# Loading order, weight piece width and one add moved between engines, at the start of a fused attention and gated-FFN kernel

## The chip, the cores and the metric

The kernel runs on one core of a Trainium2 chip. A core has a matrix engine (TensorE, PE in the profile; its weight loads are PEld), VectorE (DVE), ScalarE (ACT), GpSimd (POOL), a queue engine that issues the loads and stores (SyncE, SP), and sixteen DMA engines that carry them. The metric is the device time of one execution in microseconds; lower is better. The time before is 222.35 us, the median of 3 runs (222.17 to 222.53).

## The reference

The input is 2048 tokens of 512 features, in bf16. It is normalized over the features, and two branches read the result: linear attention with 32 heads of 16, whose queries and keys go through a small matrix per head and a pair of softmaxes, and a gated bilinear feed-forward net with 1792 hidden features. The output is the input plus both branches.

```python
xn = _layernorm(x, axis=-1)
return x + _A_ref(xn, A_wqkv, A_w_phi, A_wo) + _B_ref(xn, B_w_gate, B_w_up, B_w_down)

# _A_ref
q, k, v = split(x @ wqkv)
pq, pk = q @ w_phi, k @ w_phi                    # per head, 16 x 16
phi_q = concat(softmax(pq), softmax(-pq)); phi_k = concat(softmax(pk), softmax(-pk))
kv = sum over s of phi_k^T v;  z = sum over s of phi_k
o = (phi_q @ kv) / (phi_q @ z + 1e-6)
return o @ wo

# _B_ref
return ((x @ w_gate) * (x @ w_up)) @ w_down
```

## The kernel before

Tokens are worked on in 16 tiles of 128; four tiles make a group. The 512 features are four chunks of 128, and a product over the features is four matmuls that add up in one PSUM bank. There are six banks in rotation for all short-lived results (`bank`), and a bank that is asked for waits for whoever still reads its last content.

The order of instructions on each engine is the order in which the code issues them (`manual_schedule`): nothing is reordered, and an instruction that waits holds all that stand behind it on its engine. All loads are issued on the sync queue at the top (L84 to L99), in the order written there. A load may not be issued before the one eight places ahead of it has landed.

The part that the change touches is the start, where the first group of tiles (0 to 3, tokens 0 to 511) goes through:

- Statistics and scaling on VectorE: `first_stats` computes a tile's sums (`bn_stats`, L155), then, where `amid` names a tile, scales that tile (`first_apply`, L171), and then makes mean and variance (`bn_aggr`, L347). `ln_rstd` adds epsilon to the variance (L164) and raises it to the power -0.5 (L166), both on GpSimd. The order on VectorE is: sums 0, aggregate 0, sums 1, aggregate 1, scale 0, sums 2, scale 1, aggregate 2, sums 3, scale 2, aggregate 3, scale 3, and then `make_bd` (L221), which needs the small matrices `wphi`.
- `lt(n)` transposes a scaled tile on TensorE (four transposes, L213), and ScalarE copies it to `xnT` (L215; in two halves for tiles 0 and 1).
- `vproj(n)` multiplies a tile with `wv` (L240, the result is called pv). Its first two matmuls need the first half of `wv`, the others the second half; between the halves, `amid` lets the transposes of another tile in. ScalarE evicts the results of tiles 0 and 1 (L322), VectorE those of tiles 2 and 3.
- `unit(T, f, lo, hi)` makes one chunk f of 128 hidden features for the tokens lo to hi of group T: four matmuls with `wg` into a bank g, four with `wu` into a bank u (L275); ScalarE casts g to bf16 (L279), VectorE multiplies u with it (L280). At the start, units 0 and 1 are made in two halves of 256 tokens, since only tiles 0 and 1 are there at first. From then on a unit covers 512 tokens.

TensorE's order at the start is: 10 matmuls on zeros, transposes 0, one more on zeros, half of pv 0, transposes 1, the other half, pv 1, transposes 2, unit 0 (tokens 0 to 255), half of pv 2, transposes 3, the other half, unit 1 (tokens 0 to 255), pv 3, the second halves of units 0 and 1, unit 2, the fold of `wphi` into the key weights (L231), and further units with the key products between them.

The weights `wg` and `wu` are loaded in slices of columns: `dma_gu(lo, hi)` loads chunks lo to hi of both. A slice of 256 columns is carried in pieces of 512 bytes, one of 512 columns in pieces of 1 KB.

Of the kernel before, what the change touches and what calls it, by code (L numbers as in the profile page):

```python
# [8 lines left out]
BF16 = mybir.dt.bfloat16  # L9
F32 = mybir.dt.float32  # L10
AF = mybir.ActivationFunctionType
ALU = mybir.AluOpType
# [9 lines left out]
def kernel(  # L22
# [12 lines left out]
    nc = tc.nc  # L35
    P = 128
    S, D = A_x.shape[-2], A_x.shape[-1]
# [4 lines left out]
    DC = D // P  # L42
    FC = F // P
    EPS = 1e-5
    GT = 4
    NGRP = NT // GT
    TT = GT * P
# [16 lines left out]
    wv = wpool.tile([P, DC, D], BF16)  # L64
    wphi = consts.tile([P, DC, DH], BF16)
    wg = wpool.tile([P, DC, F], BF16)
    wu = wpool.tile([P, DC, F], BF16)
# [6 lines left out]
    def dma_x(lo, hi):  # L74
        nc.sync.dma_start(out=xall[:, lo:hi, :], in_=x_view(lo, hi))

    def dma_cols(eng, w, src, lo, hi, at=0):
        eng.dma_start(out=w[:, :, lo - at:hi - at], in_=src[:, lo:hi].rearrange("(c p) f -> p c f", p=P))

    def dma_gu(lo, hi):  # L80
        dma_cols(nc.sync, wg, B_w_gate, lo * P, hi * P)
        dma_cols(nc.sync, wu, B_w_up, lo * P, hi * P)

    dma_x(0, 1)  # L84
    dma_x(1, 2)
    dma_x(2, 4)
    for lo in (0, 2):
        nc.sync.dma_start(out=wv[:, lo:lo + 2, :],
                          in_=A_wqkv[lo * P:(lo + 2) * P, 2 * D:3 * D].rearrange("(c p) f -> p c f", p=P))
    dma_gu(0, 2)  # L90
    nc.sync.dma_start(out=wphi[:], in_=A_w_phi.rearrange("(c h) d f -> (h d) c f", c=DC))
    dma_gu(2, 4)
    nc.sync.dma_start(out=wT2[:, 1, :, :], in_=A_wqkv[:, D:2 * D], transpose=True)
    dma_gu(4, 9)
    dma_x(4, 8)
# [29 lines left out]
    xnT = xpool.tile([P, DC, S], BF16)  # L125
# [15 lines left out]
    gpool = ctx.enter_context(tc.tile_pool(name="gpool", bufs=3))  # L141
# [6 lines left out]
    def bank(name, dt=F32, n=TT):  # L148
        return ps_s.tile([P, n], dt, name=name, tag="s")
# [9 lines left out]
        stats = ln_sums(n)  # L159
        nc.vector.bn_aggr(out=mv, in_=stats[:])  # L160

    def ln_rstd(mv, k):
        ve = lnpool.tile([P, GT], F32, name="ve")
        nc.gpsimd.tensor_scalar(out=ve[:, 0:k], in0=mv[:, 0:k, 1], scalar1=EPS, scalar2=None, op0=ALU.add)  # L164
        rstd = lnpool.tile([P, GT], F32, name="rstd", bufs=GT)
        nc.gpsimd.tensor_tensor(out=rstd[:, 0:k], in0=ve[:, 0:k], in1=mhalf[:, 0:k], op=ALU.pow)  # L166
        return rstd
# [70 lines left out]
    def proj(ps, n, w, js=range(DC)):  # L238
        for j in js:
            nc.tensor.matmul(ps, lhsT=xnT[:, j, n * P:(n + 1) * P], rhs=w[:, j, :],  # L240
                             start=(j == 0), stop=(j == DC - 1))

    def features(n, w, name):
        pf = bank(name)
        proj(pf, n, w)
        e = epool.tile([P, NG, 2, 4 * DH], F32, name="e")
        pfv = pf.rearrange("p (g c) -> p g c", g=NG)
        nc.scalar.activation(out=e[:, :, 0, :], in_=pfv, func=AF.Exp, scale=1.0)  # L248
        nc.scalar.activation(out=e[:, :, 1, :], in_=pfv, func=AF.Exp, scale=-1.0)  # L249
        ev = e[:].rearrange("p g s (h f) -> p (g s h) f", f=DH)  # L250
        sums = epool.tile([P, 2 * H], F32, name="sums")
        nc.vector.tensor_reduce(out=sums[:], in_=ev, axis=AX.X, op=ALU.add)  # L252
        rs = epool.tile([P, 2 * H, 1], F32, name="rs")
        nc.vector.reciprocal(out=rs[:].rearrange("p a b -> p (a b)"), in_=sums[:])  # L254
        phi = epool.tile([P, NG, P], BF16, name=f"phi{name}")
        nc.gpsimd.tensor_tensor(out=phi[:].rearrange("p g (x f) -> p (g x) f", f=DH), in0=ev,  # L256
                                in1=rs[:].to_broadcast((P, 2 * H, DH)), op=ALU.mult)
        return phi
# [6 lines left out]
    hTs = {}  # L265
    units = [(T, f) for T in range(NGRP) for f in range(FC)]

    def unit(T, f, lo=0, hi=TT):
        if T not in hTs:
            hTs[T] = hpool.tile([P, FC, TT], BF16, name="hT", tag="h")  # L270
        pss = []
        for w, name in ((wg, "g"), (wu, "u")):
            ps = bank(name)[:, 0:hi - lo]
            for c in range(DC):
                nc.tensor.matmul(ps, lhsT=w[:, c, f * P:(f + 1) * P], rhs=xnT[:, c, T * TT + lo:T * TT + hi],  # L275
                                 start=(c == 0), stop=(c == DC - 1))
            pss.append(ps)
        g_sb = gpool.tile([P, TT], BF16, name="g_sb")
        nc.scalar.copy(out=g_sb[:, 0:hi - lo], in_=pss[0])  # L279
        nc.vector.tensor_tensor(out=hTs[T][:, f, lo:hi], in0=pss[1], in1=g_sb[:, 0:hi - lo], op=ALU.mult)  # L280

    def ffn(k):
        for _ in range(k):
# [27 lines left out]
    with tc.tile_pool(name="ps_k", bufs=1, space=PSUM) as ps_k:  # L311
        kvps = [ps_k.tile([P, 4, 4, E1], F32, name=f"kv{b}") for b in range(2)]
        phiks = {}

        def vproj(n, copy=nc.scalar.copy, amid=None, later=False):
            ps = bank("pv")
            proj(ps, n, wv, range(2))
            if amid is not None:
                amid()
            proj(ps, n, wv, range(2, DC))  # L320
            def evict():
                copy(out=vts[n % NV][:, :, :, 0:DH], in_=ps.rearrange("p (a b c) -> p a b c", a=8, b=4))  # L322
            if later:
                return evict
            evict()

        def kproj(n):
            phiks[n] = features(n, W1k, "k")

        def kv(n):  # L330
            vt, phik = vts[n % NV], phiks[n]
            for gr in range(NG):
                nc.tensor.matmul(kvps[gr // 4][:, gr % 4, :, :].rearrange("p a b -> p (a b)"),  # L333
                                 lhsT=phik[:, gr, :], rhs=vt[:, gr, :, :].rearrange("p a b -> p (a b)"),
                                 start=(n == 0 and gr % 4 == 0), stop=(n == NT - 1 and gr % 4 == 3))

        mvs = [mv_tile() for n in range(GT)]
        rstds = []

        def first_apply(n):  # L340
            ln_apply(n, mvs[n][:, 0, 0:1], rstds[n][:, 0:1])

        def first_stats(n, amid=None):
            stats = ln_sums(n)
            if amid is not None:
                first_apply(amid)
            nc.vector.bn_aggr(out=mvs[n][:, 0, :], in_=stats[:])  # L347
            rstds.append(ln_rstd(mvs[n], 1))

        first_stats(0)  # L350
        first_stats(1)
        first_apply(0)
        first_stats(2, amid=1)
        first_stats(3, amid=2)
        first_apply(3)
        make_bd()
        nc.gpsimd.tensor_tensor(out=M4[:], in0=BO[:, 0:4, :], in1=BO[:, 4:8, :], op=ALU.add)
        lt(0, parts=2)
        warm_up(1)
        vproj(0, amid=lambda: lt(1, parts=2))  # L360
        copy_v = vproj(1, later=True)
        lt(2)
        copy_v()
        unit(0, 0, 0, 2 * P)
        vproj(2, copy=nc.vector.tensor_copy, amid=lambda: lt(3))
        unit(0, 1, 0, 2 * P)
        vproj(3, copy=nc.vector.tensor_copy)
        for f in range(2):
            unit(0, f, 2 * P, TT)
        del units[0:2]  # L370
        ffn(1)
        for j0 in (0, 2):
            fold(1, W1k, j0, (nc.scalar.copy, nc.vector.tensor_copy))
        ffn(1)
        ln_block(4)
        ffn(1)
        chore(2)
        kproj(0)
        ffn(1)
        chore(2)  # L380
        ffn(1)
        chore()
        kproj(1)
        ffn(1)
        chore()
        ffn(1)
        kproj(2)
        chore()
        ffn(1)
        kv(0)  # L390
        chore()
        ffn(1)
        kproj(3)
        chore()
        ffn(1)
        kv(1)
        nc.sync.dma_start(out=wT2[:, 0, :, :], in_=A_wqkv[:, 0:D], transpose=True)
        for n in range(GT, NT):
            if n in (4, 8):
                ln_block(n + 4)  # L400
            vproj(n)
            kproj(n)
            chore(1 if n % GT < 2 else 0)
            ffn(1)
            kv(n - 2)
            chore((1, 2, 2, 2)[n % GT])
            if n >= 8 and n % 2 == 0:
                qproj((n - 8) // 2)
            if n == 6:
                fold(0, W1q, 0)  # L410
            ffn(1)
            if n == 6:
                fold(0, W1q, 2)
        ffn(1)
        kv(NT - 2)
        ffn(1)
        kv(NT - 1)
        for b in range(2):
            nc.vector.tensor_tensor(out=KV[:, 4 * b:4 * b + 4, :, :], in0=kvps[b][:],
                                    in1=_bcast_ap(M4[:], [M4[:].ap[0], [0, 4], [E1, 4], [1, E1]]), op=ALU.mult)  # L420
        qproj(4)
        ffn(1)
# [64 lines left out]
```

## Time and profile before

The profiled execution took 221.94 us, of which 220.2 are the span from the first to the last instruction.

| | before |
|---|---|
| median of 3 runs, us | 222.35 (222.17 to 222.53) |
| profiled execution, us | 221.94 |
| its span, us | 220.2 |
| TensorE busy, 0 to 5 us | 3.76 of 5.00 |
| TensorE busy, 5 to 10 us | 4.56 of 5.00 |
| TensorE busy, 10 to 16 us | 5.95 of 6.00 |
| TensorE busy, 16 to 25 us | 8.95 of 9.00 |
| TensorE busy, 100 to 150 us | 49.68 of 50.00 |
| mean granted TensorE clock | 0.998 |

The rows of stages come from a view that sums the busy time of each engine between two times. TensorE's matmuls overlap, and their ends are modelled in the trace, so distances are better measured from start to start. Times in all views are microseconds from the start of the span. In the timeline views a row is a group of like instructions in a row; its second column is the length of the whole group. A landing is the time from the issue of a load until its last part has reported.

### The profile page before, as it was taken

To read this page: it belongs to the slowest core of one execution; us is meant where nothing else is said; L and a number is where in the kernel's file an instruction comes from. 1 tells how busy PE (TensorE), PEld (TensorE's weight loads), DVE (VectorE), ACT (ScalarE), POOL (GpSimd) and SP (SyncE) were. 2 spreads that over 40 slices of the span, in tenths; PEclk is the share of its full clock that TensorE was granted. 3 is DMA by queue.
4 is the path that set the end of the run, shared out by engine and by line. 5 is a ranking of instruction groups with operands and counts; after the bars stand their busy time and mean duration, and the time that the engine had idled before them with its cause. 6 is when DMAs were issued, how large, how long until landed. Compare 5 with 4: busy or idle time off the path is not lost.

```text
span 220.2 us, 3489 instructions
## 1 busy us (share of the span) xinstructions
PE 214.5 (97%) x1285; PEld 104.4 (47%) x1309; DVE 138.4 (63%) x237; ACT 88.2 (40%) x162; POOL 72.1 (33%) x62
## 2 busy tenths in 40 slices
PE   7999999999999999999999999999999999999995
PEld 2564444445444444444544444444444444454443
DVE  5657985885579685756589964197655745445321
ACT  2635486559755876545354221231322323100000
POOL 5300555455336653536333633033033033000000
PEclk9999999999999999999999999999999999999999
DMA  5999994404201223010205945214431431522611
GB/s 171 261 306 383 368 225 59 95 1 49 49 0 33 42 54 65 18 34 0 48 1 100 119 95 113 58 24 95 98 72 24 95 71 27 91 53 71 69 30 48
DMA packets 47233, 19.91 MB, mean 90 GB/s; under 512 B 37488, under 2 KB 46960, under 8 KB 47088
## 3 DMA queue, kind: packets, MB, share of 16 engines
q1 hardware_dynamic: 47216, 19.69, 39.6%
q8 instruction: 10, 0.16, 0.3%
q14 instruction: 7, 0.06, 0.1%
HBM read 8.67 MB, written 2.10 MB: 49 GB/s over the span
## 4 chain that ended last, share of the span: by engine, by line
PE 94%; DVE 2%; DMA 1%; issue 1%; POOL 0%; ACT 0%; DVEq 0%
PE fin L293 22%; PE u L275 22%; PE g L275 21%; PE fin L296 6%; PE pv L240 6%; PE q L240 6%; PE k L240 6%; PE ab L430 2%; PE kv L333 2%; DMA xall<-in_A_x_dram 1%; DVE stats L155 1%; PE pq L231 1%; DVE sums L252 1%; PE tp L213 0%; DVE hT L280 0%
## 5 line engine op out<-in xcount | busy, mean ns | idle before, releaser
L275 PE MATMUL u<-xnT,wu 128*128 128x512 bf16 (+1 forms) x229 | 57.7, 372 | 0.4
L275 PE MATMUL g<-xnT,wg 128*128 128x512 bf16 (+1 forms) x222 | 56.7, 371 | 0.4
L280 DVE TENSOR_TENSOR hT<-u,g_sb 128x512 bf16<-128x512 f32 (+1 forms) x58 | 37.4, 649 | 27.3 <-PE u L275 18.0
L279 ACT CAST g_sb<-g 128x512 bf16<-128x512 f32 (+1 forms) x58 | 33.3, 573 | 48.2 <-PE g L275 48.1
L252 DVE TENSOR_REDUCE sums<-e 128x64 f32<-128x1024 f32 x32 | 38.9, 1215 | 20.7 <-ACT e L249 20.7
L293 PE MATMUL fin<-wd,hT 128*128 128x512 bf16 (+2 forms) x234 | 50.9, 366 | 0.3
L256 POOL TENSOR_TENSOR phiq<-e,rs 128x1024 bf16<-128x1024 f32 x16 | 31.0, 1935 | 61.4 <-DVE rs L254 53.1
L256 POOL TENSOR_TENSOR phik<-e,rs 128x1024 bf16<-128x1024 f32 x16 | 30.9, 1934 | 48.2 <-DVE rs L254 46.2
L275 PEld LDWEIGHTS <-wu 128*128 128x128 bf16 x232 | 22.6, 98 | 25.7
L293 PEld LDWEIGHTS <-hT 128*128 128x128 bf16 x238 | 22.4, 98 | 24.8
L275 PEld LDWEIGHTS <-wg 128*128 128x128 bf16 x232 | 21.9, 98 | 23.4
L240 PEld LDWEIGHTS <-xnT 128*128 128x128 bf16 x192 | 17.3, 97 | 18.2 <-ACT xnT L215 1.1
L299 DVE TENSOR_TENSOR o_sb<-fin,xall 128x512 bf16<-128x512 f32 (+2 forms) x17 | 11.2, 656 | 22.3 <-PE fin L296 22.2
L248 ACT ACTIVATE e<-q 128x512 f32<-128x512 f32 x16 | 9.5, 596 | 26.1 <-PE q L240 20.7
L254 DVE RECIPROCAL rs<-sums 128x64 f32<-128x64 f32 x32 | 17.7, 553 | 3.1
L240 PE MATMUL pv<-wv,xnT 128*128 128x512 bf16 x62 | 16.4, 379 | 0.4 <-ACT xnT L215 0.2
L296 PE MATMUL fin<-wo,oT 128*128 128x512 bf16 (+2 forms) x68 | 16.6, 366 | 0.0
L240 PE MATMUL k<-W1k,xnT 128*128 128x512 bf16 x63 | 16.2, 379 | 0.0
L240 PE MATMUL q<-W1q,xnT 128*128 128x512 bf16 x60 | 15.9, 378 | 0.1
L322 ACT CAST vt<-pv 128x512 bf16<-128x512 f32 x14 | 8.3, 591 | 10.9 <-PE pv L240 10.9
L248 ACT ACTIVATE e<-k 128x512 f32<-128x512 f32 x16 | 9.6, 597 | 7.0 <-PE k L240 6.6
L439 DVE TENSOR_TENSOR otok<-ab,rden 128x512 bf16<-128x512 f32 x16 | 11.1, 691 | 0.6
(46 smaller groups left out, 117.4 us busy)
## 6 DMA issues: line engine op xcount, KB each, us to landing
out_dram<-o_sb SPq DMA_DIRECT2D x15, 128.0 KB, 1.9
wd<-in_B_w_down_dram SPq DMA_DIRECT2D x1, 1792.0 KB, 15.4
wg<-in_B_w_gate_dram SPq DMA_DIRECT2D x2, 640.0 KB, 7.0
wu<-in_B_w_up_dram SPq DMA_DIRECT2D x2, 640.0 KB, 8.1
xall<-in_A_x_dram SPq DMA_DIRECT2D x1, 1024.0 KB, 12.0
wv<-in_A_wqkv_dram SPq DMA_DIRECT2D x2, 256.0 KB, 3.9
wg<-in_B_w_gate_dram SPq DMA_DIRECT2D x2, 256.0 KB, 4.9
wu<-in_B_w_up_dram SPq DMA_DIRECT2D x2, 256.0 KB, 5.3
```

The costliest lines, as they stand in the source:

```text
L240: nc.tensor.matmul(ps, lhsT=xnT[:, j, n * P:(n + 1) * P], rhs=w[:, j, :], start=(j == 0), stop=(j == DC - 1))
L248: nc.scalar.activation(out=e[:, :, 0, :], in_=pfv, func=AF.Exp, scale=1.0)
L252: nc.vector.tensor_reduce(out=sums[:], in_=ev, axis=AX.X, op=ALU.add)
L254: nc.vector.reciprocal(out=rs[:].rearrange("p a b -> p (a b)"), in_=sums[:])
L256: nc.gpsimd.tensor_tensor(out=phi[:].rearrange("p g (x f) -> p (g x) f", f=DH), in0=ev, in1=rs[:].to_broadcast((P, 2 * H, DH)), op=ALU.mult)
L275: nc.tensor.matmul(ps, lhsT=w[:, c, f * P:(f + 1) * P], rhs=xnT[:, c, T * TT + lo:T * TT + hi], start=(c == 0), stop=(c == DC - 1))
L279: nc.scalar.copy(out=g_sb[:, 0:hi - lo], in_=pss[0])
L280: nc.vector.tensor_tensor(out=hTs[T][:, f, lo:hi], in0=pss[1], in1=g_sb[:, 0:hi - lo], op=ALU.mult)
L293: nc.tensor.matmul(ps, lhsT=hTs[T][:, f, t4 * P:(t4 + 1) * P], rhs=wd[:, f, lo:lo + w], start=(f == 0), stop=False)
L296: nc.tensor.matmul(ps, lhsT=oTs[n][:, c, :], rhs=wo[:, c, lo:lo + w], start=False, stop=(c == DC - 1))
L299: nc.vector.tensor_tensor(out=o_sb[:], in0=ps, in1=xall[:, n, lo:lo + w], op=ALU.add)
L439: nc.vector.tensor_tensor(out=o_tok[:].rearrange("p (b h d) -> p b h d", b=2, d=DH), in0=abv[:, :, :, 0:DH], in1=rden[:].to_broadcast((P, ...
```

## The change

On the sync queue, tiles 2 and 3 of x become loads of their own: tile 2 goes between the halves of `wv`, tile 3 behind the second half. The first two slices of `wg` and `wu` (256 columns each) become one of 512 columns each, and both go ahead of `wphi`. The epsilon of tile 0 is added on VectorE instead of GpSimd; the other tiles keep GpSimd. `unit` is split into `gate`, `keep` and `up`. For the first 256 tokens both g groups (units 0 and 1) now stand together ahead of pv 2, with their casts, and both u groups together behind it, each followed by its product.

```diff
+    def dma_wv(lo, hi):
+        nc.sync.dma_start(out=wv[:, lo:hi, :],
+                          in_=A_wqkv[lo * P:hi * P, 2 * D:3 * D].rearrange("(c p) f -> p c f", p=P))
+
     dma_x(0, 1)
     dma_x(1, 2)
-    dma_x(2, 4)
-    for lo in (0, 2):
-        nc.sync.dma_start(out=wv[:, lo:lo + 2, :],
-                          in_=A_wqkv[lo * P:(lo + 2) * P, 2 * D:3 * D].rearrange("(c p) f -> p c f", p=P))
-    dma_gu(0, 2)
+    dma_wv(0, 2)
+    dma_x(2, 3)
+    dma_wv(2, DC)
+    dma_x(3, 4)
+    dma_gu(0, 4)
     nc.sync.dma_start(out=wphi[:], in_=A_w_phi.rearrange("(c h) d f -> (h d) c f", c=DC))
-    dma_gu(2, 4)
     nc.sync.dma_start(out=wT2[:, 1, :, :], in_=A_wqkv[:, D:2 * D], transpose=True)
...
-    def ln_rstd(mv, k):
+    def ln_rstd(mv, k, eng=nc.gpsimd):
         ve = lnpool.tile([P, GT], F32, name="ve")
-        nc.gpsimd.tensor_scalar(out=ve[:, 0:k], in0=mv[:, 0:k, 1], scalar1=EPS, scalar2=None, op0=ALU.add)
+        eng.tensor_scalar(out=ve[:, 0:k], in0=mv[:, 0:k, 1], scalar1=EPS, scalar2=None, op0=ALU.add)
...
-    def unit(T, f, lo=0, hi=TT):
+    def half(name, w, T, f, lo, hi):
+        ps = bank(name)[:, 0:hi - lo]
+        for c in range(DC):
+            nc.tensor.matmul(ps, lhsT=w[:, c, f * P:(f + 1) * P], rhs=xnT[:, c, T * TT + lo:T * TT + hi],
+                             start=(c == 0), stop=(c == DC - 1))
+        return ps
+
+    def gate(T, f, lo=0, hi=TT):
+        ps = half("g", wg, T, f, lo, hi)
+        g_sb = gpool.tile([P, TT], BF16, name="g_sb")
+        return ps, g_sb
+
+    def keep(g, lo=0, hi=TT):
+        nc.scalar.copy(out=g[1][:, 0:hi - lo], in_=g[0])
+
+    def up(g, T, f, lo=0, hi=TT):
         if T not in hTs:
             hTs[T] = hpool.tile([P, FC, TT], BF16, name="hT", tag="h")
...
+        ps = half("u", wu, T, f, lo, hi)
+        return lambda: nc.vector.tensor_tensor(out=hTs[T][:, f, lo:hi], in0=ps, in1=g[1][:, 0:hi - lo], op=ALU.mult)
+
+    def unit(T, f, lo=0, hi=TT):
+        g = gate(T, f, lo, hi)
+        mult = up(g, T, f, lo, hi)
+        keep(g, lo, hi)
+        mult()
...
-        first_stats(0)
+        first_stats(0, eng=nc.vector)
...
-        unit(0, 0, 0, 2 * P)
+        lo = (0, 2 * P)
+        gs = [gate(0, f, *lo) for f in range(2)]
+        for g in gs:
+            keep(g, *lo)
         vproj(2, copy=nc.vector.tensor_copy, amid=lambda: lt(3))
-        unit(0, 1, 0, 2 * P)
+        for f, g in enumerate(gs):
+            up(g, 0, f, *lo)()
         vproj(3, copy=nc.vector.tensor_copy)
```

More of the change, by code (lines that the diff above doesn't have):

```diff
@@ L266 @@
     units = [(T, f) for T in range(NGRP) for f in range(FC)]
-    def unit(T, f, lo=0, hi=TT):
+    def half(name, w, T, f, lo, hi):
[11 more added lines that the diff above has]
+    def up(g, T, f, lo=0, hi=TT):
         if T not in hTs:
             hTs[T] = hpool.tile([P, FC, TT], BF16, name="hT", tag="h")
[L271 to L280, printed above, removed]
+        ps = half("u", wu, T, f, lo, hi)
[5 more added lines that the diff above has]
+        mult()
     def ffn(k):
@@ L341, in first_apply, with first_stats @@
             ln_apply(n, mvs[n][:, 0, 0:1], rstds[n][:, 0:1])
-        def first_stats(n, amid=None):
+        def first_stats(n, amid=None, eng=nc.gpsimd):
             stats = ln_sums(n)
@@ L347, in first_stats @@
             nc.vector.bn_aggr(out=mvs[n][:, 0, :], in_=stats[:])
-            rstds.append(ln_rstd(mvs[n], 1))
-        first_stats(0)
+            rstds.append(ln_rstd(mvs[n], 1, eng))
+        first_stats(0, eng=nc.vector)
         first_stats(1)
```

## The prediction

> **What bounds the kernel now.** I read the page first, for the engine that has no time to spare.
>
> ```profile
> span 220.2 us, 3489 instructions
> PE 214.5 (97%) x1285; PEld 104.4 (47%) x1309; DVE 138.4 (63%) x237; ACT 88.2 (40%) x162; POOL 72.1 (33%) x62
> ...
> PE 94%; DVE 2%; DMA 1%; issue 1%; POOL 0%; ACT 0%; DVEq 0%
> ```
>
> TensorE is busy 97% of the span and 94% of the chain. From 16 us on the windows view gives it 99% or more until the tail, and the change touches nothing there that TensorE waits for. So what counts is when its stream begins and where it breaks in the first 16 us. The chain of waits over that stretch, second (start, length, what):
>
> ```profile
> 0.79 2.09 DMA xall<-in_A_x_dram
> 2.88 0.02 issue
> 2.90 0.71 DVE stats L155
> 3.61 0.02 issue
> 3.63 0.19 DVE mv L347
> 3.82 0.08 issue
> 3.90 0.25 POOL ve L164
> 4.15 0.07 issue
> 4.22 0.59 POOL rstd L166
> 4.81 0.03 issue
> 4.84 0.42 DVE xn L171
> ...
> 6.17 0.60 PE pv L240 x2
> ```
>
> Until 6.17 one thread runs through tile 0: load, statistics, epsilon on GpSimd, power, scaling, transposes, copy. Every hundredth saved there moves the whole stream forward. Third, TensorE's timeline (start, length of the group, count at the end):
>
> ```profile
> 6.61 0.39 PE L213 MATMUL tp<-ident,xn 128*128 128x128 bf16 x4
> 6.99 1.50 PE L240 MATMUL pv<-wv,xnT 128*128 128x512 bf16 x6
> 8.34 0.39 PE L213 MATMUL tp<-ident,xn 128*128 128x128 bf16 x4
> 8.56 0.60 PE L275 MATMUL g<-xnT,wg 128*128 128x256 bf16 x4
> 8.99 0.60 PE L275 MATMUL u<-xnT,wu 128*128 128x256 bf16 x4
> ```
>
> Ends overlap, so starts count. Four transposes take 0.22 (8.34 to 8.56), four 256-wide matmuls 0.43 to 0.44 (8.56 to 8.99), a 512-wide one 0.216 (a later group of four starts 0.87 before the next). So tile 1's transposes end at 6.83 and the next matmul starts at 6.99: 0.16 lost. The six pv up to 8.34 take 1.35 where 6 x 0.216 is 1.30: 0.05 lost. The rest runs at pace.
>
> Fourth, the loads. Starts are from the sync queue's timeline, landings from the tile views: tiles 2 and 3 of x 1.71 + 3.0 = 4.7; wv halves 2.18 + 3.5 = 5.7 and 2.69 + 4.3 = 7.0 (the late matmul at 6.99 waited for this one); wg 3.20 + 4.7 = 7.9; wu 3.72 + 5.2 = 8.9; wphi 4.27 + 4.9 = 9.2. So wu landed 0.1 us before its use at 8.99. In order of bytes: 512 KB by 4.7, 768 by 5.7, 1024 by 7.0, 1280 by 7.9, 1536 by 8.9. The two DMA views below are of 7 to 10 us (512-byte and smaller pieces) and 24 to 28 us (1 KB pieces):
>
> ```profile
> DMA packets 2275, 0.80 MB, mean 267 GB/s; under 512 B 906, under 2 KB 2275, under 8 KB 2275
> ```
>
> ```profile
> DMA packets 1349, 1.41 MB, mean 352 GB/s; under 512 B 1, under 2 KB 1345, under 8 KB 1345
> ```
>
> **The change, part by part.**
>
> *Epsilon on VectorE, tile 0.* Removed from the chain: ve and its two hand-overs, 0.08 + 0.25 + 0.07 = 0.40. Added: a hand-over within VectorE (0.02, as at 3.61), the add, and one hand-over to GpSimd (0.08). A 128x1 add on VectorE is not in the trace; nearest rows are the 128x4 memset (0.06) and the 128x2 aggregate or the 128x32 add of L435 (0.18 each). So rstd starts 0.12 to 0.24 earlier and ends, with hand-over, at 4.60 to 4.72. But the add stands in VectorE's queue ahead of tile 1's statistics, and the scaling of tile 0 stands behind those. Statistics 1 move from 3.73 to 3.86 - 4.00, their aggregate from 4.42 to 4.55 - 4.69, and the scaling follows that by 0.10 at the earliest (as statistics follow the aggregate at 3.63): 4.65 to 4.79 instead of 4.84. Gain 0.05 to 0.19; I take **0.12**, the middle, since the two nearest rows lie at the two ends. Tile 1's epsilon starts up to 0.2 later, which its transposes cover (next part).
>
> *Order of x and wv.* The queue now carries x0, x1, wv half, x2, wv half, x3: one issue more ahead of the weights (0.41 to 0.47 each). Bytes land in the order of the queue, so by the row above: first wv half 4.7, x2 (640 KB) 5.2, second half (896 KB) halfway from 5.7 to 7.0, 6.35, x3 7.0.
> The second half no longer holds TensorE: wanted at 6.83 - 0.12 = 6.71, there at 6.35. Yet the 0.16 isn't won. Tile 1's first product needs that tile's copies, which follow its transposes and allowed 7.46 before; with everything 0.12 earlier they allow 7.34. TensorE reaches it at 6.71 + 0.43 = 7.14 and waits 0.20 there. The stall moves from a load to ScalarE; gain beyond the 0.12: **0**.
> x2 at 5.2 delays statistics 2 (5.16) by 0.05 to 0.1; scaling 1 behind them on VectorE ends about 6.25, its transposes are due at 6.49. x3 at 7.0 moves statistics 3 from 6.17 to 7.03, and the scaling of tile 2 stands behind them: 7.64, done 8.05 (7.66 before). Its transposes are due at 8.34 - 0.12 = 8.22, hand-over 0.05: covered by 0.12. Scaling 3 comes 1.49 after scaling 2, as now (7.25 to 8.74), ends 9.54, due about 9.74. So **0**, and lost beyond x3 at 7.12.
>
> *Weights in 512 columns, gates first.* TensorE's instructions are the same in number and size. Two g groups now stand at 8.56 - 0.12 = 8.44 and need all 512 KB of wg, 1536 KB in all; before, 1280 KB were enough for g at 8.56 and 1536 KB for u at 8.99. The demand is earlier by 0.55 for the same bytes. Against it stands the piece: 1 KB instead of 512 bytes. From x3 at 7.0, 512 KB (524 kB) take 1.49 at 352 GB/s and 1.96 at 267: landing 8.5 or 9.0 (and 8.9 by the same bytes before). The lower end: x3 lands 0.37 behind the second wv half (128 KB at 352), at 6.72, and wg goes at the 369 GB/s of the stretch from 3.5 to 4.5 us: 8.1. Nearest is the row of the same piece size behind the landing that these bytes had, so 8.5. A matmul starts 0.04 after a landing (6.95, 6.99), so the stall is 8.54 - 8.44 = **0.10**, bounds 0 and 0.55.
>
> The Trainium skill, "DMA: Bandwidth & Descriptors", section Specifications, gives 512 bytes as the smallest transfer at line rate. By it the wider pieces win nothing, and the landing is that of the same bytes, 8.9: a stall of 0.5 instead of 0.1, the sum +0.4. Between 7 and 10 us, 906 of 2275 packets are under 512 bytes, so the trace doesn't settle it. I stay with the rows.
>
> wu follows wg by 1.49 to 1.96 and is wanted 0.87 + 0.43 + 0.22 + 0.43 = 1.95 after g (two g groups, half of pv, transposes, half of pv): about 0 either way. wphi goes behind twice the weights, to some 10.2; bd waits for it on VectorE (9.19 before, the very moment it landed), with the eviction of pv 2 (10.72) and the products behind it. Their VectorE work of the old 10.14 slot has moved behind the second u, so bd at 10.2 + 0.44 = 10.64 is just clear; later, it would hold the banks that those evictions free. ScalarE does two g casts (0.39 each) ahead of tile 3's copy: at 9.60, 9.98, copy 10.24 to 10.83, its matmul due at about 11.3. Cost **0**. The transposing load of wT is issued earlier (about 5.3 instead of 7.02) and isn't wanted before the fold at 15.82.
>
> *Sum.* -0.12 (epsilon) + 0 + 0.10 (wg) = -0.02 us. The profiled execution took 221.94 (220.2 of span and 1.74 around it), so 221.92; the runs' median is 222.35, 0.41 above it. I put the difference on the median and round: **222.3**.
>
> **The rivals.**
> *A, wg late.* The first gate is the point at which a single late engine of the sixteen stops TensorE. It decides from 8.96 on: stall 0.56, less 0.12, is 0.44, that is 0.2% of the median, about what a measurement of this kernel tells from no change. For it: same bytes, 8.9; 267 GB/s, 9.0; wv's second half took 1.3 for 256 KB. Against it: 352 GB/s with 1 KB pieces. At 9.1: +0.58, 222.95.
> *B, x3 late.* Beyond 7.12 the transposes of tile 2 wait for scaling 2. At 7.5: 0.38 - 0.12, 222.6. Against: 1024 KB were there by 7.0.
> *C, faster by more than the thread.* The ordinary run is 0.41 slower than the profiled one; if that is a longer wait for wv and wu at 6.99 and 8.99 than this trace shows, the new order takes most of it away: 222.35 - 0.12 - 0.35 = 221.9. Nothing in the trace places those 0.41.
> *D, the epsilon does nothing.* If the add takes 0.2 on VectorE, statistics 1 push the scaling back to 4.84: +0.10 of wg alone, 222.45.
>
> **How the numbers follow.** Forecast (-0.35 to +0.35 around the median) 0.56; A 0.20; B 0.06; C 0.08; D 0.10. Within 0.2%: 0.56 + 0.06 + 0.10 = 0.72; slower 0.20; faster 0.08. The range runs from 221.95, where C begins, to 222.9, inside A: below it is C (0.08), above it about half of A (0.10). The forecast alone: 222.0 to 222.7.
>
> **What would show it.** Right: ve on VectorE at 3.85, scaling 0 at 4.65 to 4.79, first pv at 6.05; no stall on wv but one of 0.2 before tile 1's product; first g at 8.45 to 8.6, from then on TensorE's old pace with the same offset to the end. Wrong: first g after 8.9, transposes of tile 2 later than 8.3, a gap before u, or an offset that grows after 16 us.

## The result, and the profile after

The changed kernel is slower: 223.24 us (222.72 to 223.64, 6 runs) against 222.33 us (222.17 to 222.53, 6 runs) of the kernel before, a ratio of 1.004 with a 95% interval of 1.0027 to 1.0054. The profiled execution took 223.48 us.

The page, and then the chain of waits up to 16 us, of the changed kernel:

```profile
span 221.8 us, 3488 instructions
PE 214.9 (97%) x1285; PEld 104.5 (47%) x1309; DVE 138.5 (62%) x238; ACT 88.1 (40%) x162; POOL 71.9 (32%) x61
```

```profile
3.67 6.50 DMA wg<-in_B_w_gate_dram
10.18 0.05 issue
10.22 1.05 PE g L274 x8
11.27 0.43 PE pv L243 x2
```

Where the chain ran through tile 0's normalization before, it now runs through one load: the 512 KB slice of wg, issued at 3.67, landed at 10.18, and the first gate started 0.04 later. TensorE's timeline shows how it came to that (last column: idle before, and what ended it):

```profile
6.08 0.61 PE L243 MATMUL pv<-wv,xnT 128*128 128x512 bf16 x2 [0.25 <-ACT xnT L218]
6.52 0.39 PE L216 MATMUL tp<-ident,xn 128*128 128x128 bf16 x4
6.75 1.66 PE L243 MATMUL pv<-wv,xnT 128*128 128x512 bf16 x6
9.46 0.40 PE L216 MATMUL tp<-ident,xn 128*128 128x128 bf16 x4 [1.05 <-DVE xn L174]
10.22 1.05 PE L274 MATMUL g<-xnT,wg 128*128 128x256 bf16 x8 [0.36 <-DMA wg<-in_B_w_gate_dram]
```

The stream starts 0.09 earlier than before (6.08, was 6.17), and the second half of wv doesn't hold it in this trace (6.75 follows the four transposes at once). Then it breaks twice: the transposes of tile 2 start at 9.46 instead of 8.34, and the first gate at 10.22 instead of 8.56, which is 1.66 late. The span is longer by 1.6 (221.8, was 220.2): what was lost by 10.2 us is still lost at the end, and next to nothing was lost after. VectorE shows why the transposes were late:

```profile
6.28 0.17 DVE L363 BATCH_NORM_AGGREGATE mv<-stats 128x2 f32<-128x6 f32 x1
8.40 0.69 DVE L158 BATCH_NORM_STATS2 stats<-xall 128x6 f32<-128x512 bf16 x1 [1.94 <-DMA xall<-in_A_x_dram]
9.01 0.40 DVE L174 TENSOR_SCALAR xn<-xall,mv,rstd 128x512 bf16<-128x512 bf16 x1
```

The statistics of tile 3 waited 1.94 for x3, which landed at 8.38, and the scaling of tile 2 (9.01), whose data had long been there, stood behind them.

### The profile page after: what moved, and what is told of

The parts are those of the page before. It is cut to its first block, busy times and chain, and to the rows that moved or that the text cites. A ratio compares the mean times of both kernels' runs of the same rounds, so it can differ in the third digit from the quotient of the medians.

```text
span 221.8 us, 3488 instructions
## 1 busy us (share of the span) xinstructions
PE 214.9 (97%) x1285; PEld 104.5 (47%) x1309; DVE 138.5 (62%) x238; ACT 88.1 (40%) x162; POOL 71.9 (32%) x61
## 4 chain that ended last, share of the span: by engine, by line
PE 92%; DMA 3%; DVE 2%; SPq 1%; issue 1%; DVEq 0%
PE fin L309 22%; PE u L274 22%; PE g L274 21%; PE fin L312 6%; PE q L243 6%; PE k L243 6%; PE pv L243 5%; DMA wg<-in_B_w_gate_dram 3%; PE ab L450 2%; PE kv L349 2%; SPq L75 1%; PE pq L234 1%; DVE sums L255 1%; SPq L85 0%; DVE hT L290 0%
## 5 line engine op out<-in xcount | busy, mean ns | idle before, releaser
L158 DVE BATCH_NORM_STATS2 stats<-xall 128x6 f32<-128x512 bf16 x16 | 10.7, 670 | 3.1 <-DMA xall<-in_A_x_dram 3.0
```

What stands on the lines that cost most here:

```text
L158: nc.vector.bn_stats(out=stats[:], in_=xall[:, n, :])
```

## The experiments

Each run stands beside runs of the kernel before on the same chip; ratios are to those, with 95% intervals. Times in the traces are of one execution each. "e5" and the like are short for the runs' labels. "Narrow" slices have 256 columns (512-byte pieces), "wide" ones 512 columns (1 KB pieces); x2 and x3 are the loads of tiles 2 and 3 of x.

| run | x and wv | first weight slices | other | median us | ratio | interval |
|---|---|---|---|---|---|---|
| e2 | new | narrow | gate, up in turn; add on GpSimd | 222.66 | 1.0019 | 1.0011 to 1.0028 |
| e3 | old | wide | | 222.96 | 1.0032 | 1.0021 to 1.0044 |
| e4 | new | narrow | | 222.40 | 1.0003 | 0.9994 to 1.0012 |
| e5 | old | narrow | | 222.35 | 1.0004 | 0.9995 to 1.0013 |
| e6 | new | wide | wT later | 222.93 | 1.0030 | 1.0018 to 1.0043 |
| e7 | new | narrow | wT earlier | 222.40 | 1.0001 | 0.9991 to 1.0010 |
| e8 | old | wide | wT later | 222.81 | 1.0025 | 1.0014 to 1.0036 |
| e9 | old | narrow | 9 matmuls on zeros | 222.23 | 0.9996 | 0.9987 to 1.0004 |
| e10 | new | 512-byte pieces, all of wg first | | 223.09 | 1.0038 | 1.0024 to 1.0052 |
| e11 | new | wide | the changed kernel again | 223.08 | 1.0037 | 1.0024 to 1.0049 |
| e12 | new | narrow | 9 matmuls on zeros | 222.29 | 1.0007 | 0.9998 to 1.0015 |
| e13 | new | narrow | e12, scaling 2 ahead of statistics 3 | 222.29 | 1.0002 | 0.9993 to 1.0011 |

From e3 on, every run has the gates first and tile 0's add on VectorE.

### Which part costs

e2 is the kernel before with the new order of x and wv alone:

```diff
-    dma_x(2, 4)
...
+    dma_wv(0, 2)
+    dma_x(2, 3)
+    dma_wv(2, DC)
+    dma_x(3, 4)
```

> The kernel before with the new order of x and wv alone. Theory 1 (x3 lands late behind the second wv half, statistics 3 wait for it, and scaling 2 stands behind them): x3 lands after 7.5, statistics 3 start with the landing instead of at 6.17, the transposes of tile 2 start about 1.1 us after the landing, 8.7 or later instead of 8.34, and the time is 0.4 to 1.1 us above before. Theory 2 (the 512 KB slice of wg is what is late, x3 in the changed kernel was late by chance): within 0.2 us of before.

e3 is the changed kernel with the old order of x and wv:

```diff
-    dma_wv(0, 2)
-    dma_x(2, 3)
+    dma_x(2, 4)
+    dma_wv(0, 2)
     dma_wv(2, DC)
-    dma_x(3, 4)
```

> The changed kernel with the old order of x and wv (tiles 2 and 3 in one load ahead of wv); wide slices, gates first and the add on VectorE stay. Theory 1: no wait for x at statistics 3, transposes of tile 2 at 8.2 to 8.3; what is left is a wait for wg of 0 to 0.6 us, so 222.2 to 222.8. Theory 2: first gate matmul at 9.5 or later, 223 or more.

e4 is the changed kernel with slices of 256 columns:

```diff
-    dma_gu(0, 4)
+    dma_gu(0, 2)
     nc.sync.dma_start(out=wphi[:], in_=A_w_phi.rearrange("(c h) d f -> (h d) c f", c=DC))
+    dma_gu(2, 4)
```

> The changed kernel with the weight slices of 256 columns as before (two units' gates need 256 KB of wg, not 512); new x order, gates first and the add on VectorE stay. Theory 1: statistics 3 and the transposes of tile 2 are as late as in the changed kernel, the first gate follows them without a wait of its own, 222.8 to 223.2. Theory 2: 222.2.

e5 has both of these edits, so that all loads are as before.

> All loads as before; gates first and the add on VectorE stay. Both theories: the thread of tile 0 is 0.1 shorter, wu is wanted 1 us later, so no wait on a load after the second wv half: 0.1 to 0.15 us below before, 222.2.

The dividing line is the width: wide slices cost 0.32% with the old order of x (e3) and 0.4% with the new one, narrow slices with the gates first leave no difference that these runs can tell from zero (e4, e5). The gain of 0.1 to 0.15 us that was expected of e5 didn't show either. So theory 1 fell as the main account: taking the order of x back (e3) took little of the loss away. In e4's trace the first gate follows the transposes of tile 2 without a wait:

```profile
6.58 0.73 PE L244 MATMUL pv<-wv,xnT 128*128 128x512 bf16 x2
7.14 0.39 PE L217 MATMUL tp<-ident,xn 128*128 128x128 bf16 x4
7.37 1.66 PE L244 MATMUL pv<-wv,xnT 128*128 128x512 bf16 x6
8.87 0.39 PE L217 MATMUL tp<-ident,xn 128*128 128x128 bf16 x4
9.09 1.04 PE L275 MATMUL g<-xnT,wg 128*128 128x256 bf16 x8
```

e2 did cost 0.19%, at the lower end of theory 1, but its trace puts the break elsewhere: statistics 3 did wait for x3 (landed 7.36), the transposes of tile 2 came at 8.59 behind a pv group that kept TensorE busy until then, and the wait stands before u:

```profile
8.59 0.39 PE L217 MATMUL tp<-ident,xn 128*128 128x128 bf16 x4
8.81 0.60 PE L279 MATMUL g<-xnT,wg 128*128 128x256 bf16 x4
9.55 0.61 PE L279 MATMUL u<-xnT,wu 128*128 128x256 bf16 x4
```

Four matmuls of 256 columns take 0.44, so u was due at 9.25 and started at 9.55, with the landing of wu at 9.50. Where the gates come first (e4), u isn't due until 11, and that wait is gone.

### Is it the transposing load behind?

With wide slices the transposing load of wT is issued at 5.25 and its issue ends only at 11.62 (before: 7.02 to 10.51). e6 moves it behind the next slices, in the changed kernel; e8 does so in e3.

```diff
     nc.sync.dma_start(out=wphi[:], in_=A_w_phi.rearrange("(c h) d f -> (h d) c f", c=DC))
-    nc.sync.dma_start(out=wT2[:, 1, :, :], in_=A_wqkv[:, D:2 * D], transpose=True)
     dma_gu(4, 9)
+    nc.sync.dma_start(out=wT2[:, 1, :, :], in_=A_wqkv[:, D:2 * D], transpose=True)
```

> The changed kernel with the transposing load of wT issued behind the next slices (chunks 4 to 9 of wg and wu) instead of ahead of them. Theory 3 (wide slices are few descriptors, so the transposing load gets into the queue at 5.2 instead of 7.0 and slows some DMA engines while x3, wg and wu are still under way): the last engine's part of wg lands within 0.7 us of the median one, x3 before 7.5, first gate at 8.5 to 8.9, 222.3 to 222.7, unless the fold then waits for wT (due at about 16). Theory 4 (the 1 KB pieces of the weights themselves, or the 512 KB on which the first gate hangs, are slow on some engines whatever comes behind): first gate after 9.3, 222.9 or more.

> e3 (wide slices, old x order, gates first, add on VectorE) with the transposing load of wT behind chunks 4 to 9. Theory 3: first gate at 8.4 to 8.8 (if the clock is up early), 222.1 to 222.5. Theory 4: as e3, first gate about 1 us late, 222.9.

e7 does the opposite in e4, where the slices are narrow:

```diff
     nc.sync.dma_start(out=wphi[:], in_=A_w_phi.rearrange("(c h) d f -> (h d) c f", c=DC))
-    dma_gu(2, 4)
     nc.sync.dma_start(out=wT2[:, 1, :, :], in_=A_wqkv[:, D:2 * D], transpose=True)
+    dma_gu(2, 4)
```

> e4 (narrow slices, new x order, gates first, add on VectorE) with the transposing load of wT moved ahead of the second pair of narrow slices, so that it is issued at 5.2. Theory 3: some engines fall behind as in the changed kernel: last part of x3 after 7.5, of wu after 9.8, time at least 0.4 us above e4, 222.8 or more. Theory 4: landings of x3, wg and wu as in e4, and the time of e4, unless the second slices, wanted at 14, come too late behind wT, which would show as a wait at unit 2 alone.

All three speak against theory 3. Without the early transposing load the first gate still came at 9.64 (e6) and 9.50 (e8), and the time stayed 0.30% and 0.25% up; with it, narrow slices stayed where they were (1.0001).

### Piece size or bytes

e10 loads the same 512 columns in 512-byte pieces, and both slices of wg first, so that the first gate hangs on 512 KB as in the changed kernel.

```diff
-    dma_gu(0, 4)
+    for w, src in ((wg, B_w_gate), (wu, B_w_up)):
+        for lo in (2, 0):
+            dma_cols(nc.sync, w, src, lo * P, (lo + 2) * P)
```

> The changed kernel with the 512 columns of wg and of wu carried in 512-byte pieces: both slices of wg, the one that the first gates need second, then both of wu. The first gate hangs on the same 512 KB as in the changed kernel, and only the size of the pieces differs. Theory 5 (wide pieces are slow on a few engines): the last part of wg lands 1.8 to 2.0 us after the last part of x3, with the twelfth and the fifteenth engine no further apart than they were for x3; first gate 0.4 us or more earlier than in the changed kernel, 222.5 to 222.9. Theory 6 (the price is that of the bytes on which the gate hangs, at any size of piece): first gate as in the changed kernel, 223.1 to 223.3.

e11 is the changed kernel unaltered, for a second trace on the same chip.

> The changed kernel unaltered, for a second trace beside the others on one chip. If x3 at 8.38 was one late engine by chance, x3 lands at 7.4 to 7.6 here and wg at 9.5 or later all the same, so that the wait moves from the transposes of tile 2 to the first gate, and the time stays at 223.2. If x3 is late by rule, it lands after 8 again.

The time of theory 6: 1.0038 and 1.0037. Theory 5 fell, although a part of it showed: a few engines are late. A load has landed when all sixteen engines have reported their part. In e10 the fifteenth of the sixteen engines reported x3 0.40 after the twelfth, and the last slice of wg 0.61; in the first trace of the changed kernel it was 0.48 and 1.16. But it doesn't move the time. e10 and e4 have pieces of the same size, the same order of x and the same work, and differ in what lies in front of the first gate, 512 KB or 256 KB of wg: 1.0038 against 1.0003, some 0.8 us. The other loads that stand later in e10 (wu, wphi, wT) held nothing up in its trace: u follows pv 2 at once, at 11.88, and the span is 1.4 longer than before, where the first gate is 1.35 late. In that trace the first 256 KB of wg landed at 8.97 and the second, which the gate needs, at 9.86. The first gate in e10 and then in e11, with e11's chain behind it:

```profile
9.18 0.40 PE L218 MATMUL tp<-ident,xn 128*128 128x128 bf16 x4 [0.38 <-DVE xn L176]
9.91 1.05 PE L276 MATMUL g<-xnT,wg 128*128 128x256 bf16 x8 [0.33 <-DMA wg<-in_B_w_gate_dram]
```

```profile
6.67 1.66 PE L243 MATMUL pv<-wv,xnT 128*128 128x512 bf16 x6
8.31 0.40 PE L216 MATMUL tp<-ident,xn 128*128 128x128 bf16 x4
9.38 0.83 PE L274 MATMUL g<-xnT,wg 128*128 128x256 bf16 x6 [0.68 <-DMA wg<-in_B_w_gate_dram]
```

```profile
3.67 5.66 DMA wg<-in_B_w_gate_dram
9.34 0.05 issue
```

In e11 x3 landed at 7.22 and held the transposes of tile 2 by no more than 0.14 (they start at 8.31, and the six pv ahead of them take 1.50 where nothing waits, as in e4); they end at 8.53, and the gate waits until 9.38: 0.85 for wg alone. Its span is 220.9, 0.7 above before, though the stream began 0.17 earlier (6.00). So the wait takes either form: for x3 first and less for wg behind it, or all of it for wg.

### What hides the add, and the queue behind x3

e9 is e5 with one matmul on zeros fewer, e12 is e4 with the same, e13 is e12 with the scaling of tile 2 ahead of the statistics of tile 3 (the lines behind the dots, in e13 alone).

```diff
-    warm_up(10)
+    warm_up(9)
...
-        first_stats(3, amid=2)
+        first_apply(2)
+        first_stats(3)
```

> e5 (old loads, gates first, add on VectorE) with 9 instead of 10 matmuls on zeros ahead of tile 0's transposes; the output is not touched by them. In executions whose clock rises late, the ten matmuls end at 5.48, later than tile 0 is scaled, and hide what the add on VectorE gains. If that is so, the first transposes start at 5.2 in either kind of execution and the time falls by 0.1 to 0.25 against e5, to 222.1 to 222.2. Rival: with less work the clock rises later, and the time is that of e5 or longer.

> New order of x and wv, gates first, add on VectorE, narrow slices as before, and 9 instead of 10 matmuls on zeros. If narrow slices leave the first gate without a wait, and the second wv half no longer holds tile 0's product: 222.0 to 222.2, at or below e9. If x3 holds the transposes of tile 2: 222.3 to 222.5.

> e12 with the scaling of tile 2 ahead of the statistics of tile 3 on VectorE, so that it no longer stands behind the load of x3. If that queue is the price of the new x order, the transposes of tile 2 start at 8.0 to 8.4 even where x3 lands after 7.5, and the time is at or below e12, 222.0 to 222.2, unless the later statistics 3 now hold the transposes of tile 3 (due about 9.8). If the new x order costs through the landings of wg alone, the time stays that of e12.

TensorE in e9, to be compared with e4 above (transposes of tile 0 at 5.48, first pv at 6.58):

```profile
5.17 0.61 PE L216 MATMUL tp<-ident,xn 128*128 128x128 bf16 x4
5.58 0.63 PE L323 MATMUL warm<-zeros 128*128 128x512 bf16 x1
6.25 0.74 PE L243 MATMUL pv<-wv,xnT 128*128 128x512 bf16 x2
```

In both traces the matmuls are still slow here (the groups of transposes take 0.61 and 0.63, where 0.40 is usual), and with nine the first pv starts 0.33 earlier. Other traces with slow matmuls at the start give less: 6.35 with nine (e12), 6.42 to 6.58 with ten (e2, e3, e6, e8). The runs give 0.9996 for e9 and 1.0004 for e5, with intervals that overlap, so a gain was seen in the traces and isn't shown in the time. In e13 the scaling of tile 2 came ahead of x3, which landed at 7.55:

```profile
7.47 0.41 DVE L175 TENSOR_SCALAR xn<-xall,mv,rstd 128x512 bf16<-128x512 bf16 x1 [1.00 <-POOL rstd L170]
7.80 0.69 DVE L159 BATCH_NORM_STATS2 stats<-xall 128x6 f32<-128x512 bf16 x1
```

The transposes of tile 2 started at 8.51, on time behind pv, while in e12 they waited until 9.17 with x3 at 8.08 (1.09 after it). The queue behind x3 is real, then. The time shows no gain from lifting it: 1.0002 for e13 and 1.0007 for e12, each against the kernel before on its own chip, with intervals that overlap. Statistics 3 came later themselves in e13 (tile 3's transposes 0.13 late). None of the versions beats the kernel before by more than its interval; e9 comes nearest.

## Why the prediction was wrong, point by point

The sum was -0.02 us, and +0.91 was measured, median against median. Nearly all of the difference lies in one term, the landing of wg.

- **The add on VectorE: right.** From landing of x0 to the first pv it was 3.29 (2.88 to 6.17) and is 3.16 (2.92 to 6.08): 0.13, forecast 0.12. The forecast took for granted that TensorE is free then. In executions like e4's it isn't: the matmuls on zeros run to 5.48, and the transposes could have started at 5.2 (the scaling of tile 0 ends at 5.13).
- **wv: right for the changed kernel's two traces, with less to spare than forecast.** No wait for its second half; 0.20 lost ahead of tile 1's product instead (7.37 against 7.18), forecast 0.20. But that half landed at 6.68 and 6.58, hardly 0.1 ahead of its use, where 6.35 was forecast. Over the nine traces with the new order it landed between 6.50 and 7.31, and in e7, e10 and e13 TensorE waited 0.23, 0.37 and 0.30 for it.
- **x3: right mechanism, late by half a microsecond.** Forecast 7.0, with 7.12 as the point from which it costs. It landed at 8.38, and at 7.22 in e11; over the nine traces with the new order between 6.87 and 8.38, with 7.55 in the middle. Where they waited for it (the changed kernel, e10, e12), the transposes of tile 2 came 1.08 to 1.09 after the landing; the forecast's own steps make it 1.10.
- **wg: the step that failed.** The term of the sum is the landing of wg: 1.49 after x3, at 8.5, a stall of 0.10 with an upper bound of 0.55. Measured from x3's landing to wg's: 1.80 and 2.12 in the two traces of the changed kernel, 2.01 in e6, and 1.77 in e10 with 512-byte pieces. wg landed at 9.34 to 10.18 in these four, and the stall was 0.85 where x3 left it alone (e11). The mechanism was right and the size wrong: with e11's landing the prediction's own sum is 9.38 - 8.44 - 0.12 = 0.82. On the profiled execution of the kernel before that makes 222.76, and e11's took 222.68; on the median it makes 223.17, and 223.24 and 223.08 were measured. Two mistakes lie in the size.

  The 352 GB/s was a mean over the sixteen engines, from a stretch without such a wait; a load has landed when the last engine has. In e11 the ninth of the sixteen engines reported at 8.34, close to the forecast, and the last at 9.34. From the ninth report of x3 to the ninth of wg it was 1.44 and 1.65 in the changed kernel's traces and 1.43 in e6, about as forecast, but 1.80 in e10. So the wider pieces were quicker on the middle engine and not on the last one, which decides. Why a few engines fall behind stays open.

  The other mistake is the landing "of the same bytes before", 8.9, which was taken as the nearest thing to a worst case. It is the earliest of all fourteen traces. The same 1536 KB landed at 8.92, 9.10 and 9.16 with the old loads (before, e5, e9), at 9.18 to 9.84 with narrow slices and the new order, which has one more load ahead of them, and at 9.34 to 10.18 with wide ones (9.46 and 9.69 with the old order of x; 9.86 in e10).
- **The rule.** The Trainium skill, "DMA: Bandwidth & Descriptors", section Specifications, gives 512 bytes as the smallest transfer at line rate. The times agree: with the same order of x and wv and 512 KB ahead of the gate, 512-byte and 1 KB pieces cost the same (1.0038 and 1.0037, each known to some 0.0014). The prediction's sum by the rule, +0.4, was the better one and still too small, since it rested on the old landing of 8.9.
- **u, bd, the casts: right that they cost nothing; wphi's landing was wrong.** No gap before u (12.19, at once behind pv 2). wphi was put at 10.2 and landed at 11.88, and bd started at 11.90, past the 10.64 of the forecast. It did no harm here, with TensorE itself 1.66 late by then.
- **Rivals.** A, which had a chance of 0.20, came true, with B in front of it in the profiled execution: x3 at 8.38 and wg at 10.18. Both waits are for the same queue of bytes, so they don't add up; the later landing decides. C didn't come true (no version is clear of its interval on the fast side), nor did D (the thread got 0.13 shorter).

## What to carry to other kernels

Ask of a load not only when it lands but how many bytes its first reader hangs on: merging two slices into one made the first gate wait for twice what it reads. Price a landing by the slowest engine in a row of landings, not by a mean rate, where the reader is due within some tenths of it, and by more than one trace where there is one: the landing of 8.9 turned out to be the earliest of fourteen. And where several landings lie close to their readers, an edit of the order moves the wait rather than removing it.

## What the runs showed of the hardware

TensorE's start comes in two kinds. In the changed kernel's trace the matmuls on zeros go from a spacing of 0.43 to 0.29 and less at 4.6 to 4.9, and the transposes of tile 0 start at 5.22. In e2, e3, e4, e6 and e8 the spacing of 0.43 lasts to 5.48, and in e3, e4, e6, e9 and e12 the transposes of tile 0 are still slow as well (0.11 from start to start, where 0.06 is usual). The views give the granted clock as 1.00 in either case. The record of the clock in the packed traces does tell the two apart. The full clock begins there at 4.41 in the kernel before, at 4.78 in the changed kernel, at 4.24 in e11 and at 3.94 to 4.58 in e7, e10 and e13. In e2, e3, e4, e6, e8, e9 and e12 it begins at 5.65 to 7.04. (e5 has no such record; its spacing changes at 4.6.) The Trainium skill, "TensorE: Matmul & The Clock Gate", Part 1, says why: a free-running window raises the clock, so the moment differs from run to run. The traces agree in that the moment differs, by up to 3.1 us; no run here shows the window itself. First pv at 6.0 to 6.2 in one kind and at 6.4 to 6.6 in the other (with ten matmuls on zeros) is a difference of about 0.4 us, the size of the 0.41 between the profiled execution of the kernel before and its median. That this is the cause there wasn't shown: no trace of the kernel before with a late clock was taken.
